# Four changes of order in a fused attention and GELU-MLP kernel: a value load, one set of transposes, a batch's loads and its row sums

## The chip, the cores and the metric

The kernel runs on one core of a Trainium2 chip. The metric is device time in microseconds (us) of one launch. The core's engines are TensorE (PE, matrix multiplication; its weight loads are shown as PEld), VectorE (DVE), ScalarE (ACT), GpSimd (POOL) and SyncE (SP). SP issues most of the DMAs, POOL those that change the type on the way.

## The reference, cut to what matters

```python
batch, n_heads, seq, head_dim = (8, 12, 448, 64)          # q, k, v in float32
q_n, k_n = (rmsnorm(q, g_q), rmsnorm(k, g_k))             # x / sqrt(mean(x*x) + 1e-6) * g
scores = (1.0 / np.sqrt(64)) * np.matmul(q_n, k_n.transpose(0, 1, 3, 2))
attn = softmax(scores)                                    # sum + 1e-9 in the divisor
x = np.matmul(attn, v).transpose(0, 2, 1, 3).reshape(3584, 768)
h = x @ w_in                                              # w_in 768 x 2048
g = gelu_tanh(h)
out = g @ w_out                                           # w_out 2048 x 768, float32
```

## The kernel before, in words

**Tiling.** A batch has 448 rows (4 groups of 112) and 12 heads, treated as 6 *pairs* of heads (two heads fill 128 lanes) and as 3 *chunks* of 4 heads. Batches are counted from 0 here, as in the code: "batch 1" of the change's short name is batch 0, its "batch 2" is batch 1, its "batch 3" is batch 2. `(b, c)` below is chunk c of batch b.

**Stages.** For each batch q and k are loaded chunk by chunk (`loads(b, c)`: one DMA for q, one for k, issued by SP, 448 KB each). The squares are made (`square`, on POOL or ACT), summed along each head's 64 elements (`total`, a DVE reduction), turned into 1/rms (`rsqrt` on ACT, or `rsqrt_pow` with a power on POOL), multiplied in (`normed`, on POOL or DVE), and transposed so that the head's 64 elements lie on the lanes. Transposing goes through TensorE and two DVE copies (`trans`, whole batch 0 and chunk 0 of batch 1), or through a DMA transpose that SP issues (`transposed(b, c)`: one for q, one for k), after which DVE multiplies the gain into the keys (`gain`). Buffers for q and k rotate over four tiles each; the squares of one tag (`sq`) over two.

**Attention of one batch** (`attention(b, ...)`) runs over 12 *slots*: slot 2p and 2p+1 belong to pair p. In a slot, the functions of a hand-written list (`side`) are issued first, then two blocks of `scores` (PE, followed by an exponential on ACT). An even slot also holds `pair_sums` of the pair before: with `what` = 0 the sums of the exponentials (PE, "ones") and their reciprocal, spread over the lanes by three DVE instructions (L253 to L255); with `what` = 1 the product with v (PE) and the scaling to x, written to `xT` (DVE, L248). Between them PE works off the second MLP multiplication of the batch before (`m2`, L283), whose results DVE copies to `osb` (L294) every 16 matmuls. At slot 11 `rsqrt` of the next batch but one is issued on ACT ahead of the slot's exponentials.

**Batch 0** has an attention of its own (`first_attention`) with four hand-written lists per slot: `side` ahead of the slot, `mid` between its two score blocks, `early` after them and ahead of `pair_sums`, `late` behind it. Here pair p+1 is transposed on PE at slot 2p+1, and one half of `pair_sums` of the pair before runs in each slot. POOL issues the loads of v (`load_v`, which converts to bf16) and the four halves of the MLP weights (`w_in_part`, `w_out_part`), between its squares and normalizations. Behind it comes the first MLP multiplication of batch 0 in pairs (`mm1_pair`, 8 steps), with its own list (`m1`, slots 0 to 7), and then `attention(1)`, whose `side` list is written in the loop's `b == 0` branch.

**Order.** Every engine works its own instructions in the order in which this program issues them; nothing is reordered by a scheduler (`manual_schedule`). An instruction that waits holds up everything behind it on its engine. A DMA starts when the issuing engine (SP or POOL) reaches it.

Of the kernel before, what the change touches and what calls it, by code (L numbers as in the profile page):

```python
# [16 lines left out]
def kernel(  # L17
# [11 lines left out]
    nc = tc.nc  # L29
# [7 lines left out]
    HP = H // 2  # L37
    CH = 4
    NCH = H // CH
# [17 lines left out]
    ps_m = ctx.enter_context(tc.tile_pool(name="ps_m", bufs=2, space=bass.MemoryType.PSUM))  # L57
# [32 lines left out]
    def load(b, c, n, parts=1, eng=nc.sync):  # L90
        t = rawqk.tile([P, CH, NK, D], F32, tag=f"raw{n}", name=f"raw{n}")
        src = {"q": q, "k": k}[n]
        raws[n, b, c] = t
        m = CH // parts
        return [
            lambda i=i: eng.dma_start(
                t[:, i * m:(i + 1) * m],
                src[b, c * CH + i * m:c * CH + (i + 1) * m].rearrange(
                    "h (p t) d -> p h t d", t=NK
                ),  # L100
            )
            for i in range(parts)
        ]

    def loads(b, c):
        for n in "qk":
            for go in load(b, c, n):
                go()

    def load_v(b, h, n):  # L110

        nc.gpsimd.dma_start(
            vb[b % 2][:, h:h + n], v[b, h:h + n].rearrange("h (p t) d -> p h t d", t=NK)
        )

    def square(b, c, n, eng, hs=slice(0, CH)):
        if (n, b, c) not in sqs:
            sqs[n, b, c] = stp.tile([P, CH, NK, D], F32, tag="sq", name="sq")
        sq, raw = sqs[n, b, c][:, hs], raws[n, b, c][:, hs]
        if eng is nc.scalar:  # L120
            nc.scalar.activation(sq, raw, AF.Square)  # L121
        else:
            eng.tensor_mul(sq, raw, raw)  # L123

    def total(b, c, n, hs=slice(0, CH)):
        if b not in sss:
            sss[b] = smp.tile([P, NCH, 2, CH, NK], F32, tag="ss", name="ss")
        nc.vector.reduce_sum(  # L128
            sss[b][:, c, "qk".index(n), hs], sqs[n, b, c][:, hs], axis=AX.X
        )  # L130
# [34 lines left out]
    def trans(b, hp, home=None):  # L165

        c, j = hp // (CH // 2), hp % (CH // 2)
        if hp == 0:
            qT[b] = qkp.tile([128, HP, S], BF16, tag="qT", name="qT")
        if home is ps_m:  # L170
            tp = ps_m.tile([128, 2, 512], BF16, tag="mm", name="tp")
        else:
            tp = ps_s.tile([128, 2, 1024], BF16, tag="sc", name="tp")
        for i, n in enumerate("qk"):
            for t in range(NK):
                nc.tensor.transpose(
                    tp[:, i, t * P:(t + 1) * P],
                    nrms[n, b, c][:, j, t].rearrange("p a d -> p (a d)"),
                    ident[:P, :P],
                )  # L180
        if b == 0 and hp == 0:
            nc.scalar.copy(qT[b][:, hp], tp[:, 0, :S])
        else:
            nc.vector.tensor_copy(qT[b][:, hp], tp[:, 0, :S])
        nc.vector.tensor_scalar(
            kT[:, hp, :, :P], tp[:, 1, :S].rearrange("p (t s) -> p t s", s=P), gcol[:, 0:1],
            None, op0=ALU.mult,
        )
# [249 lines left out]
    def pair(hp):  # L438
        return hp // (CH // 2), hp % (CH // 2), slice(2 * (hp % (CH // 2)), 2 * (hp % (CH // 2)) + 2)

    def squares0(hp, eng):
        c, _, hs = pair(hp)
        for n in "qk":
            square(0, c, n, eng, hs)

    def totals0(hp):
        c, _, hs = pair(hp)
        for n in "qk":
            total(0, c, n, hs)
# [5 lines left out]
    def normed0(hp, eng):  # L455
        c, j, _ = pair(hp)
        for n in "qk":
            normed(0, c, n, j, eng)

    def w_in_part(i, n):  # L460
        m = d_ff // n
        nc.gpsimd.dma_start(
            win[:, :, i * m:(i + 1) * m],
            moe_w_in[:, i * m:(i + 1) * m].rearrange("(c p) f -> p c f", p=128),
        )
# [34 lines left out]
    load_v(0, 0, 2)  # L500
    square(0, 1, "k", nc.gpsimd, slice(0, 2))
    load_v(0, 2, 4)
    w_in_part(0, 2)
    total(0, 1, "q", slice(0, 2))

    def pool_waits(b, c, n, j):
# [3 lines left out]
    side = [(1, lambda: normed0(1, nc.vector), lambda: pool_waits(0, 0, "k", 1),  # L510
             lambda: squares0(3, nc.gpsimd), lambda: total(0, 1, "k", slice(0, 2)),
             lambda: loads(1, 0)),
            (2, lambda: rsqrt0(2), lambda: normed0(2, nc.gpsimd),
             lambda: squares0(4, nc.gpsimd), lambda: totals0(3)),
            (4, lambda: normed0(3, nc.gpsimd), lambda: squares0(5, nc.gpsimd),
             lambda: totals0(4), lambda: loads(1, 1)),
            (6, lambda: normed0(4, nc.gpsimd), lambda: load_v(0, 6, 6),
             lambda: w_in_part(1, 2), lambda: totals0(5)),
            (8, lambda: normed0(5, nc.gpsimd),
             lambda: square(1, 0, "q", nc.gpsimd), lambda: square(1, 0, "k", nc.gpsimd),  # L520
# [2 lines left out]
             lambda: load_v(1, 0, CH), lambda: w_out_part(1)),  # L523
            (11, lambda: square(1, 1, "k", nc.gpsimd), lambda: square(1, 2, "q", nc.gpsimd))]
    mid = [(0, lambda: rsqrt0(1))] + [(2 * hp - 3, lambda hp=hp: rsqrt0(hp)) for hp in range(3, HP)]
    early = [(2 * hp + 1, lambda hp=hp: trans(0, hp + 1, ps_m)) for hp in (0, 2, 3, 4)]
    late = [(3, lambda: trans(0, 2, ps_m)), (9, lambda: total(1, 0, "q"))]
    first_attention(plan(*side), plan(*mid), plan(*early), plan(*late))
    def normed1(c):
        for j in range(CH // 2):  # L530
# [3 lines left out]
    def transposed(b, c):  # L534
        for n in "qk":
            dma_trans(b, c, n)
# [12 lines left out]
    for b in range(B):  # L549
        m1, side = [], []  # L550
        if b == 0:
            m1 = [(1, lambda: normed1(0), lambda: total(1, 1, "q"), lambda: total(1, 1, "k"),
                   lambda: load_v(1, CH, 2 * CH), lambda: rsqrt_pow(1, 1),
                   lambda: normed_all(1, 1)),
                  (2, lambda: total(1, 2, "q"), lambda: total(1, 2, "k"),
                   lambda: rsqrt_pow(1, 2), lambda: normed_all(1, 2)),
                  (3, lambda: trans(1, 0, ps_m)),
                  (4, lambda: trans(1, 1, ps_m), lambda: transposed(1, 1))]
            side += [(0, lambda: transposed(1, 2), lambda: loads(2, 0), lambda: loads(2, 1),
                      lambda: loads(2, 2)),  # L560
                     (2, lambda: gain(1, 1)), (5, lambda: gain(1, 2))]
            for c in range(NCH):
                side += [
                    (2 * c + 1, lambda c=c: square(2, c, "q", nc.gpsimd)),
                    (2 * c + 1, lambda c=c: square(2, c, "k", nc.gpsimd)),
                    (2 * c + 5, lambda c=c: total(2, c, "q")),
                    (2 * c + 6, lambda c=c: total(2, c, "k")),
                ]
        elif b + 1 < B:
            for c in range(NCH):  # L570
                m1 += [(0, lambda c=c: normed_all(b + 1, c)),
                       (4 * c + 4, lambda c=c: transposed(b + 1, c))]
            m1 += [(9, lambda: gain(b + 1, 0)), (14, lambda: gain(b + 1, 1))]
            side.append((3, lambda: gain(b + 1, 2)))
        if 0 < b and b + 2 < B:
            m1 += [(4, lambda: loads(b + 2, 1)), (8, lambda: loads(b + 2, 2))]
            for c, at in ((0, 1), (1, 9)):
                for i, (n, half) in enumerate((n, half) for n in "qk" for half in range(2)):
                    m1.append((at + i, lambda c=c, n=n, half=half: squared(b + 2, c, n, half)))
                m1 += [(at + 2, lambda c=c: total(b + 2, c, "q")),  # L580
                       (at + 4, lambda c=c: total(b + 2, c, "k"))]
            for n, slot in (("q", 1), ("k", 2)):
                m1.append((13, lambda n=n: square(b + 2, 2, n, nc.gpsimd)))
                side.append((slot, lambda n=n: total(b + 2, 2, n)))
        m1 = plan(*m1)
        for f in range(nf // 2 if b == 0 else nf):
            if b > 0:
                mm1(b, f)
            elif f > 1:
                mm1_pair(f)  # L590
            for fn in m1.get(f, ()):
                fn()
        m2 += m2_parts(b)
        if b + 1 == B:
            for fn in m2:
                fn()
            break
        nc.scalar.preload_act_table_set(EXP_SET)  # L598
        if b + 2 < B:
            side += [(11, lambda: rsqrt(b + 2)),  # L600
                     (0, lambda: load_v(b + 2, 0, H))]
            if b + 3 < B:
                side.append((1, lambda: loads(b + 3, 0)))
        attention(b + 1, m2, 96 if b == 0 else 112, plan(*side))
# [30 lines left out]
```

## Time and profile before

| | us |
|---|---|
| median of 3 runs | 454.71 (453.57 to 454.72) |
| profiled execution | 454.61 |
| its span, first to last instruction | 452.8 |
| PE busy | 433.3 (96%) |
| ACT busy | 303.6 (67%) |
| DVE busy | 249.8 (55%) |
| POOL busy | 168.3 (37%) |
| mean granted TensorE clock | 0.991 |

The time outside the span is 454.61 - 452.8 = 1.81 us. Busy time of PE contains pipelined matmuls with modelled ends, so 96% doesn't mean that PE is at its peak. A row of the timeline gives start, duration, engine, source line, operation, output<-input with its shape, count, and in brackets how long the engine stood idle just before and what released it. The rows of DMA issues give the tile, the issuing queue, the size and the time from issue to landing.

### The profile page before, as it was taken

To read this page: it belongs to the slowest core of one execution; us is meant where nothing else is said; L and a number is where in the kernel's file an instruction comes from. 1 tells how busy PE (TensorE), PEld (TensorE's weight loads), DVE (VectorE), ACT (ScalarE), POOL (GpSimd) and SP (SyncE) were. 2 spreads that over 40 slices of the span, in tenths; PEclk is the share of its full clock that TensorE was granted. 3 is DMA by queue.
4 is the path that set the end of the run, shared out by engine and by line. 5 is a ranking of instruction groups with operands and counts; after the bars stand their busy time and mean duration, and the time that the engine had idled before them with its cause. 6 is when DMAs were issued, how large, how long until landed. Compare 5 with 4: busy or idle time off the path is not lost.

```text
span 452.8 us, 7158 instructions
## 1 busy us (share of the span) xinstructions
PE 433.3 (96%) x2835; PEld 217.1 (48%) x2835; DVE 249.8 (55%) x426; ACT 303.6 (67%) x404; POOL 168.3 (37%) x142
## 2 busy tenths in 40 slices
PE   7778999799999999999999999999999999999995
PEld 3333544355445554455544554455544554555563
DVE  5777604772588436872388536873398603871000
ACT  5885469557889468856888478866888448863400
POOL 5998691873401921064400922055400910000000
PEclk9998999899999999999999999999999999999999
DMA  7999999929931768118941787217851521111022
GB/s 222 245 241 208 203 110 193 214 69 206 231 61 37 174 147 171 42 36 218 207 72 36 162 158 143 71 36 177 148 92 35 115 45 36 36 35 36 0 71 69
DMA packets 80754, 54.47 MB, mean 120 GB/s; under 512 B 39248, under 2 KB 75600, under 8 KB 80720
## 3 DMA queue, kind: packets, MB, share of 16 engines
q1 hardware_dynamic: 63936, 42.22, 39.0%
q0 software_dynamic: 16624, 11.80, 17.8%
q8 instruction: 22, 0.36, 0.3%
q14 instruction: 12, 0.10, 0.1%
q10 hardware_dynamic: 160, 0.00, 0.0%
HBM read 45.61 MB, written 11.01 MB: 125 GB/s over the span
## 4 chain that ended last, share of the span: by engine, by line
PE 73%; POOL 9%; ACT 6%; DVE 5%; DMA 3%; issue 2%; SPq 0%; ACTq 0%; DVEq 0%; POOLq 0%
PE h L262 28%; PE o L283 26%; PE o L241 11%; PE sc L214 7%; ACT ex L218 4%; DVE ss L128 3%; POOL rinv L147 2%; DMA rawk<-in_k_dram 2%; ACT L598 1%; POOL nrmk L159 1%; DVE es L229 1%; POOL g L123 1%; POOL sq L123 1%; POOL nrmq L159 1%; DMA grow<-in_g_k_dram 1%
## 5 line engine op out<-in xcount | busy, mean ns | idle before, releaser
L218 ACT ACTIVATE ex<-sc,shift 112x896 bf16<-112x896 f32 x192 | 182.7, 1003 | 32.4 <-PE sc L214 31.3
L283 PE MATMUL o<-wout,g 128*128 128x384 bf16 (+1 forms) x956 | 162.3, 329 | 0.0
L262 PE MATMUL h<-xT,win 128*128 128x448 bf16 x672 | 128.3, 352 | 0.0
L283 PEld LDWEIGHTS <-g 128*128 128x128 bf16 (+1 forms) x956 | 81.7, 99 | 71.0 <-issue 24.4
L266 ACT ACTIVATE g<-h 128x448 bf16<-128x448 f32 x112 | 60.9, 544 | 75.7 <-PE h L262 72.8
L262 PEld LDWEIGHTS <-win 128*128 128x128 bf16 x672 | 65.8, 98 | 61.0
L159 POOL TENSOR_TENSOR nrmq<-rawq,rinv 112x512 bf16<-112x512 f32 x44 | 46.8, 1082 | 127.1 <-issue 122.8
L128 DVE TENSOR_REDUCE ss<-sq 112x16 f32<-112x1024 f32 (+1 forms) x44 | 49.6, 1142 | 62.2 <-ACT sq L121 58.2
L294 DVE COPY osb<-o 128x384 f32<-128x384 f32 x52 | 28.7, 552 | 81.9 <-PE o L283 81.9
L214 PE MATMUL sc<-qT,kT 64*128 64x448 bf16 x384 | 58.0, 360 | 4.7 <-ACT ex L218 2.2
L241 PE MATMUL o<-ex,vb 112*64 112x448 bf16 x384 | 45.4, 356 | 4.0 <-DMA vb<-in_v_dram 3.3
L229 DVE TENSOR_TENSOR es<-ex 112x896 bf16<-112x896 bf16 x72 | 47.6, 662 | 2.7 <-ACT ex L218 1.7
L253 DVE STREAM_TRANSPOSE st<-o 128x448 f32<-128x448 f32 x48 | 31.1, 649 | 29.8 <-PE o L241 29.8
L159 POOL TENSOR_TENSOR nrmk<-rawk,rinv 112x512 bf16<-112x512 f32 x44 | 47.1, 1087 | 0.0
L214 PEld LDWEIGHTS <-kT 64*128 64x128 bf16 x384 | 17.3, 94 | 46.9 <-issue 40.3
L123 POOL TENSOR_TENSOR sq<-rawq 112x1024 f32<-112x1024 f32 x9 | 17.0, 1891 | 55.9 <-DMA rawq<-in_q_dram 28.3
L248 DVE TENSOR_TENSOR xT<-o,rb 128x448 bf16<-128x448 f32 x48 | 30.0, 625 | 9.3 <-PE o L241 4.7
L255 DVE STREAM_TRANSPOSE rb<-rc 128x448 f32<-128x448 f32 x48 | 31.0, 645 | 1.6
L241 PEld LDWEIGHTS <-vb 112*64 112x64 bf16 x384 | 23.2, 109 | 15.9 <-DMA vb<-in_v_dram 3.4
L241 PEld LDWEIGHTS <-ones 112*64 112x64 bf16 x240 | 15.0, 111 | 16.9 <-issue 11.2
L241 PE MATMUL o<-es,ones 112*64 112x448 bf16 x144 | 22.3, 358 | 0.6
L123 POOL TENSOR_TENSOR sq<-rawk 112x1024 f32<-112x1024 f32 (+1 forms) x11 | 19.5, 1771 | 1.9 <-POOL sq L123 0.8
(56 smaller groups left out, 216.4 us busy)
## 6 DMA issues: line engine op xcount, KB each, us to landing
rawq<-in_q_dram SPq DMA_DIRECT2D x22, 448.0 KB, 5.3
rawk<-in_k_dram SPq DMA_DIRECT2D x22, 448.0 KB, 6.2
vb<-in_v_dram POOLq DMA_DIRECT2D x6, 672.0 KB, 7.2
win<-in_moe_w_in_dram POOLq DMA_DIRECT2D x2, 1536.0 KB, 17.5
wout<-in_moe_w_out_dram POOLq DMA_DIRECT2D x2, 1536.0 KB, 19.3
out_dram<-osb SPq DMA_DIRECT2D x8, 336.0 KB, 2.8
out_dram<-osb SPq DMA_DIRECT2D x8, 288.0 KB, 2.7
out_dram<-osb SPq DMA_DIRECT2D x8, 240.0 KB, 2.7
```

Of the source, the lines that this page charges most:

```text
L123: eng.tensor_mul(sq, raw, raw)
L128: nc.vector.reduce_sum(sss[b][:, c, "qk".index(n), hs], sqs[n, b, c][:, hs], axis=AX.X)
L159: eng.tensor_mul(nrms[n, b, c][:, j].rearrange("p t a d -> p a t d"), raws[n, b, c][:, 2 * j:2 * j + 2], rinvs[b][:, c, "qk".index(n), 2 * ...
L214: nc.tensor.matmul(sc[:, a, :S], kT[r, hp, kt], qT[b][r, hp], start=True, stop=True,)
L218: nc.scalar.activation(exs[b, hp][:, kt], sc[:P, :, :S], AF.Exp, scale=scale, bias=shift)
L229: nc.vector.tensor_add(ess[b, hp][:, i], ex[:, 2 * i], ex[:, 2 * i + 1])
L241: nc.tensor.matmul(o[a * D:(a + 1) * D], vb[b % 2][:, 2 * hp + a, i] if what else ones, e[:, i, a], start=(i == 0), stop=(i == n - 1),)
L253: nc.vector.transpose(st.rearrange("p a b -> p (a b)"), o)
L255: nc.vector.transpose(oas["rb"], rc.to_broadcast([128, S // 32, 32]))
L262: nc.tensor.matmul(h[:, :S], win[:, c, f * 128:(f + 1) * 128], xT[b][:, c], start=(c == 0), stop=(c == HP - 1),)
L266: nc.scalar.activation(g[:, f, (b % 2) * S:(b % 2 + 1) * S], h[:, :S], AF.Gelu_apprx_tanh)
L283: nc.tensor.matmul(o[j * m:(j + 1) * m, :HD], g[:, f, i * 128 + j * m:i * 128 + (j + 1) * m], wout[:, f, half * HD:(half + 1) * HD], start ...
```

## The change

Four edits, all of them in hand-written lists.

1. The last six heads of batch 0's v are loaded ahead of the first half of `w_in`; that half is issued on POOL at slot 2, behind the normalization of pair 2.
2. In batch 0's attention the transposes of pair 2 are issued at slot 3 ahead of the product with v, as for the other pairs, and no longer behind it.
3. The six q and k loads of batch 2 are issued on SP at slots 5 and 6 of batch 0's first MLP multiplication, ahead of the DMA transposes of batch 1's chunk 2; before, they were issued behind these, at slot 0 of `attention(1)`. Loads and transposes share SP's queue.
4. The six `total` reductions of batch 2 are issued at slots 3, 5, 7, 9, 10 and 11 of `attention(1)`; before, at 5, 6, 7, 8, 9 and 10. The squares stay where they were (slots 1, 3, 5, on POOL).

```diff
     load_v(0, 2, 4)
-    w_in_part(0, 2)
+    load_v(0, 6, 6)
     total(0, 1, "q", slice(0, 2))
...
             (2, lambda: rsqrt0(2), lambda: normed0(2, nc.gpsimd),
-             lambda: squares0(4, nc.gpsimd), lambda: totals0(3)),
+             lambda: w_in_part(0, 2), lambda: squares0(4, nc.gpsimd), lambda: totals0(3)),
...
-            (6, lambda: normed0(4, nc.gpsimd), lambda: load_v(0, 6, 6),
+            (6, lambda: normed0(4, nc.gpsimd),
              lambda: w_in_part(1, 2), lambda: totals0(5)),
...
-    early = [(2 * hp + 1, lambda hp=hp: trans(0, hp + 1, ps_m)) for hp in (0, 2, 3, 4)]
-    late = [(3, lambda: trans(0, 2, ps_m)), (9, lambda: total(1, 0, "q"))]
+    early = [(2 * hp + 1, lambda hp=hp: trans(0, hp + 1, ps_m)) for hp in range(HP - 1)]
+    late = [(9, lambda: total(1, 0, "q"))]
...
-                  (4, lambda: trans(1, 1, ps_m), lambda: transposed(1, 1))]
-            side += [(0, lambda: transposed(1, 2), lambda: loads(2, 0), lambda: loads(2, 1),
-                      lambda: loads(2, 2)),
+                  (4, lambda: trans(1, 1, ps_m), lambda: transposed(1, 1)),
+                  (5, lambda: loads(2, 0), lambda: loads(2, 1)), (6, lambda: loads(2, 2))]
+            side += [(0, lambda: transposed(1, 2)),
                      (2, lambda: gain(1, 1)), (5, lambda: gain(1, 2))]
-            for c in range(NCH):
-                side += [
-                    (2 * c + 1, lambda c=c: square(2, c, "q", nc.gpsimd)),
-                    (2 * c + 1, lambda c=c: square(2, c, "k", nc.gpsimd)),
-                    (2 * c + 5, lambda c=c: total(2, c, "q")),
-                    (2 * c + 6, lambda c=c: total(2, c, "k")),
-                ]
+            for c, slots in enumerate(((3, 5), (7, 9), (10, 11))):
+                for n, slot in zip("qk", slots):
+                    side += [(2 * c + 1, lambda c=c, n=n: square(2, c, n, nc.gpsimd)),
+                             (slot, lambda c=c, n=n: total(2, c, n))]
```

## The prediction

> **What bounds the kernel now.** I read the page first: its chain of waits is mostly PE, with POOL, ACT, DVE and DMA together under a quarter.
>
> ```profile
> PE 73%; POOL 9%; ACT 6%; DVE 5%; DMA 3%; issue 2%; SPq 0%; ACTq 0%; DVEq 0%; POOLq 0%
> ```
>
> The edits end with batch 2's preparation, inside `attention(1)`; what comes later is only shifted by them. So I read PE's timeline up to there for its gaps, each with what ended it.
>
> ```profile
> 20.01 0.55 PE L214 MATMUL sc<-qT,kT 64*128 64x448 bf16 x4 [0.88 <-DVE kT L185]
> ...
> 34.87 1.25 PE L241 MATMUL o<-ex,vb 112*64 112x448 bf16 x8 [3.28 <-DMA vb<-in_v_dram]
> ...
> 84.29 0.95 PE L241 MATMUL o<-ex,ones 112*64 112x448 bf16 x8 [1.99 <-DVE st L253]
> 85.98 1.16 PE L241 MATMUL o<-ex,vb 112*64 112x448 bf16 x8 [0.74 <-DVE xT L248]
> ...
> 97.44 0.95 PE L241 MATMUL o<-ex,ones 112*64 112x448 bf16 x8
> ```
>
> The MLP of batch 0 lies between:
>
> ```profile
> 42.20 1.12 PE L314 MATMUL hh<-xT,win 128*128 128x448 bf16 x5
> ```
>
> Two stalls: one in batch 0's attention, on v, and one in `attention(1)`, on DVE. DVE's timeline says what DVE waited for there, and gives the step sizes I need.
>
> ```profile
> 76.88 0.44 DVE L204 TENSOR_SCALAR kT<-kT,gcol 128x896 bf16<-128x896 bf16 x1
> 80.15 1.22 DVE L128 TENSOR_REDUCE ss<-sq 112x16 f32<-112x1024 f32 x1 [2.83 <-POOL sq L123]
> 82.46 1.22 DVE L128 TENSOR_REDUCE ss<-sq 112x16 f32<-112x1024 f32 x1 [1.09 <-POOL sq L123]
> 83.59 0.64 DVE L253 STREAM_TRANSPOSE st<-o 128x448 f32<-128x448 f32 x1
> ...
> 85.84 1.21 DVE L128 TENSOR_REDUCE ss<-sq 112x16 f32<-112x1024 f32 x1
> 86.97 0.55 DVE L294 COPY osb<-o 128x384 f32<-128x384 f32 x1
> 87.43 1.21 DVE L128 TENSOR_REDUCE ss<-sq 112x16 f32<-112x1024 f32 x1
> ```
>
> From start to start: a pair's chain 2.25 us (83.59 to 85.84), a total 1.13, an osb copy 0.46. The two totals wait for POOL's squares, and those (POOL's and SP's timelines) for loads of batch 2 that SP issues behind a DMA transpose.
>
> ```profile
> 48.72 5.47 POOL L147 TENSOR_TENSOR rinv<-ms,mhalf 112x32 f32<-112x32 f32 x1 [5.47 <-DVE ms L145]
> ...
> 67.92 1.04 POOL L112 DMA_DIRECT2D vb<-in_v_dram  x1
> ```
>
> ```profile
> 58.34 1.24 SPq L199 DMA_TRANSPOSE kT<-nrmk  x1
> ...
> 68.00 1.22 SPq L199 DMA_TRANSPOSE kT<-nrmk  x1
> 69.27 0.57 SPq L96 DMA_DIRECT2D rawq<-in_q_dram  x1
> ...
> 75.94 1.50 SPq L96 DMA_DIRECT2D rawk<-in_k_dram  x1
> ```
>
> **Edits 1 and 2: v and the third pair's transposes.** The rows that price them, POOL's, DVE's and the landing times of the old v load (issued at 25.73) and of the first `w_in` half (issued at 12.23):
>
> ```profile
> 12.23 0.86 POOL L462 DMA_DIRECT2D win<-in_moe_w_in_dram  x1
> ...
> 16.24 1.03 POOL L159 TENSOR_TENSOR nrmk<-rawk,rinv 112x512 bf16<-112x512 f32 x1
> ...
> 25.73 0.83 POOL L112 DMA_DIRECT2D vb<-in_v_dram  x1
> ```
>
> ```profile
> win<-in_moe_w_in_dram POOLq DMA_DIRECT2D x1, 1536.0 KB, 18.9
> ...
> vb<-in_v_dram POOLq DMA_DIRECT2D x1, 336.0 KB, 9.1
> ```
>
> v now lands at 25.73 + 9.1 = 34.8, just when PE moves. Issued at 12.2 in `w_in`'s place it would land in the twenties, so 3.28 us goes, and the eight matmuls behind it lose 0.3 (1.25 against 0.95 at full clock). Pair 2's transposes ahead of the product with v remove the 0.88 gap, since DVE copies the keys while PE multiplies; I take 0.7, because POOL's next normalization comes 0.86 later (the `w_in` issue now stands ahead of it). Sum 4.3 us from the first stage on. Cover for `w_in`: issued near 17.3 (behind 16.24 + 1.03) with the old 18.9 it lands at 36.2; the MLP multiplication begins at 42.2 - 4.3 = 37.9. Everything up to 62 then runs 4.3 earlier, as what feeds it (DVE's normalization, then POOL's power at 48.72) follows PE and DVE.
>
> **Edits 3 and 4: loads and totals.** The old stall disappears if the loads land early: SP issues them behind T1 (the DMA transposes of batch 1's chunk 1; chunk 2's are T2), from 58.34 + 1.24 - 4.3 = 55.3 instead of 69.27. Gone would be 1.99 + 0.74 us and a slow clock. One half-us window of engine use behind the stall, with the granted clock third from its end:
>
> ```profile
> 87.00:87.50 0.50, 0.50 (x6) 0.13 (x4) 0.50 (x3) 0.00 (x0) 0.37 (x1) 0.50 1.10 242
> ```
>
> It stays at 0.50 in the windows from 87.0 to 89.5. There a run of PE takes up to twice as long; 1.4 us is my estimate for some 3 us of it, less than half as some of PE's work there waits for others. By the Trainium skill, "TensorE: Matmul & The Clock Gate", Part 1, the clock falls after an idle window of about 3.4 us; by that these two short gaps would cost their 2.73 us alone, and the trace differs: 0.50 after gaps of 1.99 and 0.74.
>
> But the loads now stand in SP's queue ahead of T2. T2's gain is issued on DVE at slot 5, in the old run at 76.88, now due at 76.88 - 4.3 = 72.6. If T2 is later, DVE stands, and behind it all of pairs 2 to 4, the totals and the `rsqrt` that ACT issues ahead of its last exponentials. So the question is when T2's keys land. DMA issues and queue traffic in windows carry it; landing times first, of the issues at 58.34, 75.94, 106.28 (a load) and 108.18 (the transpose behind it):
>
> ```profile
> kT<-nrmk SPq DMA_TRANSPOSE x1, 6.6
> ...
> rawk<-in_k_dram SPq DMA_DIRECT2D x1, 448.0 KB, 12.5
> ...
> rawk<-in_k_dram SPq DMA_DIRECT2D x1, 448.0 KB, 5.3
> ...
> kT<-nrmk SPq DMA_TRANSPOSE x1, 5.0
> ...
> kT<-nrmk SPq DMA_TRANSPOSE x1, 6.5
> ```
>
> The last is T2 itself, 68.00 + 6.5 = 74.5; T1 landed at 64.9, batch 2's last load at 88.4. At 106.28 the load landed at 111.6, the transpose behind it at 113.2, 1.6 later. Next the packets of POOL's queue (q0) and SP's (q1), in 57.5 to 59, then q1 in 59 to 65, both in 74.5 to 79.5, and q1 in 80 to 88:
>
> ```profile
> q0 software_dynamic: 514, 0.27, 130.5%
> q1 hardware_dynamic: 69, 0.02, 26.4%
> ...
> q1 hardware_dynamic: 1787, 0.44, 99.4%
> ...
> q1 hardware_dynamic: 1281, 1.27, 94.4%
> q0 software_dynamic: 285, 0.14, 20.0%
> ...
> q1 hardware_dynamic: 2013, 1.99, 108.8%
> ```
>
> *T1.* While q0 still moves weights, T1 gets 69 packets in 1.5 us, 46 per us; its bulk, 1787, moves once q0 runs dry near 59.5. Issued 4.3 earlier it is stuck all the same. Upper bound 64.9, as before. Lower bound, with the bulk behind 59.5 at the pace of a transpose alone (67 to 68, below): 61.4. By the nearest row, 4.3 us more at 46 give 200 packets, 0.6 us of a bulk that took nearly 6. So 64.3.
>
> ```profile
> q1 hardware_dynamic: 926, 0.23, 101.8%
> ```
>
> *The six loads.* Before, from T2's landing at 74.5 to 88.4, 13.9 us. New is that all of batch 2's v (672 KB, about 1340 packets, issued at 67.92 - 4.3) falls into them rather than the last 285 packets. That costs nothing by one row (q1 moved 256 packets per us beside q0, 252 alone), and by q0's own pace of 514 in 1.5 us, for some 1060 packets, 3.1. I take 0.6, near the row in which both run. They end at 64.3 + 13.9 + 0.6 = 78.8.
>
> *T2's keys* 1.6 behind that: L = 80.4. Lower bound 61.4 + 13.9 + 1.6 = 76.9, or 75.7 with six loads of 448 packets at 252 per us and 2 us of tail. Upper bound: 64.9 + 13.9 + 3.1 + 1.6 = 83.5, and 85 if T2 suffers beside v as it did in the old run (6.5 us, v issued at 67.92, against 5.0 of the one at 108.18).
>
> *From L to the end of the stage.* DVE has in order: gain 0.44, the second total, pair 2, a total, osb, pair 3, two totals, pair 4, the last total: 0.44 + 5 x 1.13 + 3 x 2.25 + 0.46 = 13.3. POOL's squares are ready in time, as each waits only for the total two before it. Then ACT:
>
> ```profile
> 93.17 0.37 ACT L137 ACTIVATE lg<-ss,eps 112x96 f32<-112x96 f32 x1 [0.46 <-DVE ss L128]
> ...
> 93.76 1.89 ACT L218 ACTIVATE ex<-sc,shift 112x896 bf16<-112x896 f32 x2
> ```
>
> 0.6 us from the total's end to the exponentials and 1.9 for two of them: 15.9 us after L. Pair 5's sums end 0.45 behind that, at L + 16.35; in the old run they ended at 97.44 + 0.95 = 98.4. So the change of time is L - 82.0, and with L = 80.4 it is -1.6. How much the first stage gains no longer matters: up to about 3 of its 4.3 us could be missing, and L would stand, because the queue sets it. Against the profiled execution, 454.61 - 1.6 = 453.0; the median stands 0.1 above that execution, so 453.1.
>
> What edit 4 adds by itself: the last total now stands behind pair 4 on DVE, so `rsqrt` and the last exponentials wait for it; without a late T2 this would cost 0.8 at pair 5's sums. Nothing else waits: POOL's normalization of batch 2 starts 1 us closer to its use, and its first transpose is held by output stores anyway.
>
> **The rivals.** *Full gain* (10%): T2 lands by 74, and both stalls go: 4.3 + 2.7 + 1.4 - 0.5 = 7.9, time 446.8. For it: alone a transpose needs one us. Against: the one at 108.18 landed only behind the load ahead of it.
>
> *Half gain* (20%): the queues share better than 46 packets per us. T1 is through by 61 to 63, v costs nothing, L = 76 to 79, change -6 to -3: 448.7 to 451.7. A rule of the Trainium skill gives this case, "DMA: Bandwidth & Descriptors", Queues, rings and completion order: an engine takes turns between queues, packet by packet. With half of the 583 packets per 1.5 us from 57.7 - 4.3 = 53.4 on, T1's 1787 end at 62.6, L is 78.7 and the time 451.4. The row of 69 against 514 speaks against it for transposes; 1281 beside 285 decides nothing.
>
> *Slower* (25%): T2 is starved beside v. v's full 3.1 us and 0.5 to 1.5 of starvation put L at 84 to 85: change +2 to +3, time 456.7 to 457.7. It decides from L = 83.4. For it: T2's 6.5 us in the old run, beside v. Against: here v has 14 us to pass ahead of T2.
>
> **How the numbers follow.** About 0.3%, 1.4 us, is what a measurement of this kernel can tell from no change. The forecast (45%) spans L from 78.9 to 83.4, the bound of faster, L = 80.6, near its middle: 23% of faster and 22% of same. With the rivals: faster 0.53, same 0.22, slower 0.25. The forecast's own range is 451.6 to 456.1. For 8 in 10 the range leaves out the full gain and the worst of starvation: 448.5 to 457.0.
>
> **What would show it.** Right: no wait for v near 31, the MLP of batch 0 beginning 4 us earlier, no wait of DVE for squares in `attention(1)`, but a DVE wait of 5 to 9 us ahead of L204 there, named a DMA; PE gaps at pair 4's scores; T2's keys landing near 80. Wrong: T2 landing by 75, or T1 by 61; wrong on the other side: a PE wait for `w_in` ahead of L314 near 38, T2 beyond 83, or the totals still waiting for POOL.

## The result, and the profile after

The changed kernel took **450.53 us** (median of 5 runs, 449.68 to 451.04), the kernel before, beside it on the same chip, 453.99 (452.68 to 454.72): a ratio of 0.9917, interval [0.9892, 0.9942], 3.5 us less. The profiled execution took 451.04 with a span of 449.3, 3.57 less than the profiled one of before.

First PE's timeline of the changed kernel, the rows that answer to those of before (start, duration, engine, line, operation, output<-input, count, and in brackets the idle time just before and its releaser):

```profile
30.47 0.95 PE L241 MATMUL o<-ex,vb 112*64 112x448 bf16 x8
...
38.88 8.29 PE L314 MATMUL hh<-xT,win 128*128 128x448 bf16 x43 [0.24 <-DVE xT L248]
...
79.02 0.55 PE L214 MATMUL sc<-qT,kT 64*128 64x448 bf16 x4 [2.27 <-DVE kT L204]
80.70 1.71 PE L241 MATMUL o<-ex,ones 112*64 112x448 bf16 x8 [1.13 <-DVE st L253]
...
92.30 1.62 PE L283 MATMUL o<-wout,g 128*128 128x384 bf16 x9 [0.61 <-DVE osb L294]
93.85 0.95 PE L241 MATMUL o<-ex,ones 112*64 112x448 bf16 x8
```

There is no wait for v at 30.47, and no wait for `w_in`. The main run of batch 0's MLP starts at 38.88; the row that answers to it in the old trace starts at 43.81:

```profile
43.81 8.29 PE L314 MATMUL hh<-xT,win 128*128 128x448 bf16 x43 [0.49 <-DVE xT L248]
```

So the first stage gained 4.9 us on PE, and the end of pair 5's sums, 98.4 before, is at 93.85 + 0.95 = 94.8: 3.6 are left. The rest went into PE's gaps in `attention(1)`: 2.27 + 1.13 + 0.61 = 4.0 us, where 1.99 + 0.74 = 2.7 stood before. DVE's timeline shows where the first of them comes from:

```profile
62.86 0.66 DVE L204 TENSOR_SCALAR kT<-kT,gcol 128x896 bf16<-128x896 bf16 x1 [1.15 <-DMA kT<-nrmk]
...
68.36 1.22 DVE L128 TENSOR_REDUCE ss<-sq 112x16 f32<-112x1024 f32 x1 [0.64 <-POOL sq L123]
...
78.51 0.45 DVE L204 TENSOR_SCALAR kT<-kT,gcol 128x896 bf16<-128x896 bf16 x1 [6.22 <-DMA kT<-nrmk]
```

DVE stands for 6.22 us ahead of the gain of chunk 2, from 72.3 on (the prediction had this turn at 72.6 and a wait of 5 to 9), as T2's keys land at 78.5. PE's gap of 2.27 us at pair 4's scores follows. The old waits for squares, 2.83 and 1.09 us, have shrunk to 0.64. ACT's timeline shows the end of the stage, where ACT waits for the last total:

```profile
91.81 0.38 ACT L137 ACTIVATE lg<-ss,eps 112x96 f32<-112x96 f32 x1 [3.58 <-DVE ss L128]
...
92.41 1.89 ACT L218 ACTIVATE ex<-sc,shift 112x896 bf16<-112x896 f32 x2
```

PE waits for the same total at its last gap, the 0.61 us above: the `osb` copy that it needs stands right behind that total on DVE. So both ways to pair 5's sums lead through DVE's list.

```profile
90.57 1.21 DVE L128 TENSOR_REDUCE ss<-sq 112x16 f32<-112x1024 f32 x1
91.70 1.01 DVE L294 COPY osb<-o 128x384 f32<-128x384 f32 x2
```

The answers on DMA issues give the landing times behind T1's keys (issued at 55.78), the last of the six loads (62.57) and T2's keys (67.70):

```profile
kT<-nrmk SPq DMA_TRANSPOSE x1, 7.1
...
rawk<-in_k_dram SPq DMA_DIRECT2D x1, 448.0 KB, 8.7
...
kT<-nrmk SPq DMA_TRANSPOSE x1, 10.8
```

That is 62.9, 71.3 and 78.5. Last the packets of the two queues in 62 to 70 and in 71 to 76:

```profile
q1 hardware_dynamic: 2817, 2.69, 110.1%
...
q0 software_dynamic: 1154, 0.59, 88.2%
q1 hardware_dynamic: 1207, 0.30, 50.0%
```

The first row is 352 packets per us, but it holds the last of T1's too; from 63 on, the loads alone ran at 342, with nothing of v beside them. T2 then ran beside all of v, in equal turns.

### The profile page after: what moved, and what is told of

Read it like the earlier page. It is cut to its first block, busy times and chain, and to the rows that moved or that the text cites. A ratio compares the mean times of both kernels' runs of the same rounds, so it can differ in the third digit from the quotient of the medians.

```text
span 449.3 us, 7158 instructions
## 1 busy us (share of the span) xinstructions
PE 432.5 (96%) x2835; PEld 217.4 (48%) x2835; DVE 251.9 (56%) x426; ACT 303.7 (68%) x404; POOL 168.8 (38%) x142
## 4 chain that ended last, share of the span: by engine, by line
PE 70%; POOL 12%; DVE 7%; ACT 4%; DMA 4%; issue 2%; SPq 0%; DVEq 0%; POOLq 0%
PE h L262 28%; PE o L283 25%; PE o L241 10%; PE sc L214 7%; DVE ss L128 4%; POOL g L123 3%; POOL rinv L147 2%; DMA kT<-nrmk 2%; ACT ex L218 2%; POOL nrmk L159 2%; POOL nrmq L159 2%; ACT L596 1%; POOL sq L123 1%; DVE es L229 1%; DMA rawq<-in_q_dram 1%
## 5 line engine op out<-in xcount | busy, mean ns | idle before, releaser
L159 POOL TENSOR_TENSOR nrmq<-rawq,rinv 112x512 bf16<-112x512 f32 x44 | 46.9, 1083 | 126.8 <-issue 123.0
L159 POOL TENSOR_TENSOR nrmk<-rawk,rinv 112x512 bf16<-112x512 f32 x44 | 47.1, 1089 | 0.0
L214 PEld LDWEIGHTS <-kT 64*128 64x128 bf16 x384 | 17.4, 93 | 48.8 <-issue 40.3
```

What stands on the lines that cost most here:

```text
L159: eng.tensor_mul(nrms[n, b, c][:, j].rearrange("p t a d -> p a t d"), raws[n, b, c][:, 2 * j:2 * j + 2], rinvs[b][:, c, "qk".index(n), 2 * ...
L214: nc.tensor.matmul(sc[:, a, :S], kT[r, hp, kt], qT[b][r, hp], start=True, stop=True,)
```

## The experiments

All runs are compared with the kernel before on their own chip (medians of 453.48 to 453.71 there). L is, as in the prediction, the landing of T2's keys.

**Each pair of edits alone.** The kernel before with edits 1 and 2 (first stage) in one run, with edits 3 and 4 (loads and totals) in the other; their diffs are the two halves of the change's own.

> Kernel before with edits 1 and 2 alone (v and the third pair's transposes); batch 2's loads and totals stay as before. In the trace after, batch 0's MLP began 4.9 us earlier and POOL's power 2.6 us earlier. My theory (the end of the stage is set by the landing of the DMA transposes of batch 1's chunk 2 in the changed kernel, and by POOL's squares in this one): the wait for v is gone, the DVE wait for squares stays at 2 to 4 us and moves 2.6 to 4.9 us earlier, so the time falls by 2.6 to 4.5 us, about as much as with all four edits (3.5). Rival (edits 3 and 4 bring most of the 3.5 us): at most -1.5 us here.

> Kernel before with edits 3 and 4 alone (loads of batch 2 ahead of the transposes, one total per division); v lands late as before. My theory (the stage ends 16.35 us after L, the landing of chunk 2's transposed keys, and L hangs on the queues, not on when PE arrives): the wait for v of 3.3 us stays, chunk 1's transposes land at 63 to 65, L is 78.5 to 80.5 and the time falls by 1.5 to 3.5 us. Rival (the first stage's gain is what is seen at the end, and edits 3 and 4 trade one stall for an equal one): 0 +- 1 us here.

Edits 1 and 2 alone: 451.82, ratio 0.9959 [0.9942, 0.9976], 1.9 us. DVE's and PE's rows:

```profile
77.30 1.22 DVE L128 TENSOR_REDUCE ss<-sq 112x16 f32<-112x1024 f32 x1 [4.62 <-POOL sq L123]
79.31 1.22 DVE L128 TENSOR_REDUCE ss<-sq 112x16 f32<-112x1024 f32 x1 [0.79 <-POOL sq L123]
...
81.14 1.70 PE L241 MATMUL o<-ex,ones 112*64 112x448 bf16 x8 [3.70 <-DVE st L253]
```

That is less than the 2.6 to 4.5 expected and a little over the rival's 1.5. Part of the first stage's gain went into the old stall: DVE's first wait for squares grew from 2.83 to 4.62 and PE's gap from 1.99 to 3.70.

Edits 3 and 4 alone: 450.8, ratio 0.9938 [0.9918, 0.9957], 2.8 us.

```profile
35.08 1.33 PE L241 MATMUL o<-ex,vb 112*64 112x448 bf16 x6 [3.20 <-DMA vb<-in_v_dram]
...
78.36 0.45 DVE L204 TENSOR_SCALAR kT<-kT,gcol 128x896 bf16<-128x896 bf16 x1 [0.63 <-DMA kT<-nrmk]
...
94.00 0.95 PE L241 MATMUL o<-ex,ones 112*64 112x448 bf16 x8
```

The wait for v is still there, and yet T2 lands at 78.3, as in the full change (78.5), and the times agree within their spread. The two halves don't add: with both, what the first stage gains becomes DVE's wait for T2, 0.63 here and 6.22 there. The queue sets L, not the first stage. The run doesn't show that L sets the end: PE, which comes late here, has no gap from pair 4's scores to pair 5's sums, so its own work ends at the same place, 94.95, as L + 16.6.

**What holds T2 up.** Two kernels on the base of the change, and one with both edits. Batch 2's v behind T2:

```diff
-                      (0, lambda: load_v(b + 2, 0, H))]
+                      (8 if b == 0 else 0, lambda: load_v(b + 2, 0, H))]
```

> Changed kernel, with batch 2's v issued on POOL at slot 8 of attention(1) instead of slot 0, so that it moves after the transposes. In the trace after, the six loads had moved by 70 and the transposes of chunk 2 moved from 70 to 77 beside v's packets, one for one. Theory A (v beside the transposes makes them late): they land at 72 to 73, the DVE wait ahead of the gain (6.2 us) falls under 1.5 us, pair 5's sums end near 89.5 instead of 94.8, the time falls to 8 to 9 us under the kernel before. Rival B (the loads ahead of them in SP's queue make them late): they land at 77 or later, the wait stays over 4 us, time as the changed kernel within 1 us. Rival C (DVE's list of totals is the limit, whatever the transposes do): wait gone, but time within 1.5 us of the changed kernel.

Four of the six loads behind T2:

```diff
-                  (5, lambda: loads(2, 0), lambda: loads(2, 1)), (6, lambda: loads(2, 2))]
-            side += [(0, lambda: transposed(1, 2)),
+                  (5, lambda: loads(2, 0))]
+            side += [(0, lambda: transposed(1, 2), lambda: loads(2, 1), lambda: loads(2, 2)),
```

> Changed kernel, with only chunk 0's two loads of batch 2 ahead of the transposes of batch 1's chunk 2, the other four behind them as before; v at slot 0 as in the change, totals as in the change. Rival B (the loads ahead make the transposes late): they land by 69 to 70, no DVE wait ahead of the gain, totals of chunk 1 and 2 just in time, time 7 to 9 us under the kernel before. Theory A (v beside the transposes makes them late): they start before v's first packets at 70, so they are through by 70 here too, and the time is the same 7 to 9 under, unless the four loads beside v come too late for the squares, which would show as a DVE wait for POOL at slots 9 to 11 of 1 to 4 us. Rival C (DVE's list of totals is the limit): within 1.5 us of the changed kernel.

> Changed kernel with both moves: four of batch 2's six loads behind the transposes of batch 1's chunk 2, and batch 2's v at slot 8. Nothing lies ahead of these transposes but two loads, and nothing beside them. Theory A (the stage ends 16.4 us after the later of their landing and the gain's turn): they land at 67 to 69, DVE doesn't wait for them, the gain comes at its turn near 72.2 (73.1 with v alone moved), pair 5's sums end near 88.6, time 0.5 to 1 us under the kernel with v alone moved (7.8 us under before). Rival D (the loads' slow pace of 250 packets per us in the kernel before, against 345 in the changed one, comes with standing behind a transpose): the four loads move at 230 to 260 per us here too. Theory E (the slow pace comes when v's packets stretch the end of the transpose ahead of the loads): 330 to 350 here.

| kernel | us | ratio | T2's keys land | pair 5's sums end |
|---|---|---|---|---|
| changed | 450.53 | 0.9917 [0.9892, 0.9942] | 78.5 | 94.8 |
| v behind | 445.71 | 0.9827 [0.9811, 0.9844] | 73.0 | 89.4 |
| four loads behind | 446.92 | 0.9848 [0.9828, 0.9868] | 72.4 | 89.8 |
| both | 445.83 | 0.9831 [0.9811, 0.9851] | 67.7 | 89.2 |

With v behind, T2's packets in 71 to 72 and DVE's gain:

```profile
q1 hardware_dynamic: 1092, 0.27, 128.4%
...
73.08 0.45 DVE L204 TENSOR_SCALAR kT<-kT,gcol 128x896 bf16<-128x896 bf16 x1 [1.16 <-DMA kT<-nrmk]
...
88.42 0.95 PE L241 MATMUL o<-ex,ones 112*64 112x448 bf16 x8
```

1092 packets in one us, against 241 per us beside v: **v beside T2 was worth 5.5 us of L**, and 4.8 of the time by the medians, 4.1 by the ratios ((0.9917 - 0.9827) x 454). The end keeps its distance, 89.37 - 73.0 = 16.4. Either edit removes most of the wait, though the time fell by 7.8 us with v behind, where 8 to 9 was expected, and by 6.6 with four loads behind, where it was 7 to 9: there DVE waits 0.93 us for a square, as the late loads feed POOL late. With both, T2 lands 5 us earlier still and nothing follows, where 0.5 to 1 us was expected. L is then no longer the bound, since DVE reaches the gain only at 71.6; the rule of the fixed distance ends near L = 73.

In the run with both, the four late loads have no v beside them either and still went at about 250 packets per us (1762 in 68 to 75), where the changed kernel's went at 342. So v doesn't explain the two paces of loads of the same shape.

```profile
q1 hardware_dynamic: 1762, 1.75, 106.0%
```

**The totals.** The changed kernel with the totals at their old slots 5 to 10, and the version with both edits above with the totals at 3, 5, 7, 8, 9 and 10.

> Changed kernel with the totals of batch 2 at the old slots (5 to 10) and all else as changed: edit 3 without edit 4. Theory A (DVE's list from the landing at 78.4 on sets the stage): the first total joins the list (+1.1 us) and pair 4 leaves it ahead of the last total (-2.3), so ACT's rsqrt comes 1.1 us earlier and the time is 0.5 to 1.1 us under the changed kernel, unless PE's own work behind pair 3 holds pair 5's sums. Rival F (one total per slot is what makes the changed kernel fast): 1 us or more slower than the changed kernel.

> The kernel with both moves and the last totals earlier: slots 3, 5, 7, 8, 9, 10, so that ACT's rsqrt doesn't stand behind pair 4's chain on DVE. Theory A: the 3.3 us for which ACT waits for the last total in the kernels with v moved shrink to under 1.5, pair 5's sums follow PE's own work, the time is 0 to 0.8 us under the kernel with both moves. Rival G (the squares come too late for totals at slots 8 to 10): DVE waits 1 to 2 us for POOL there and the time is 0.5 us or more over it.

With old slots: 451.63, ratio 0.996 [0.9942, 0.9977], 1.1 us above the changed kernel as rival F had it, and not below it as theory A had it. T2 lands at 77.2, 1.3 earlier, but the sums end at 95.2, L + 18.0, 0.4 later.

```profile
77.25 0.45 DVE L204 TENSOR_SCALAR kT<-kT,gcol 128x896 bf16<-128x896 bf16 x1 [5.10 <-DMA kT<-nrmk]
...
77.76 0.55 PE L214 MATMUL sc<-qT,kT 64*128 64x448 bf16 x4 [0.88 <-DVE kT L204]
80.57 1.71 PE L241 MATMUL o<-ex,ones 112*64 112x448 bf16 x8 [2.25 <-DVE st L253]
```

Two totals now stand between the gain and the `st` that PE waits for, and PE's second gap is 2.25 instead of 1.13. ACT's last wait is gone, yet that pays nothing. The clock also fell for longer. Busy time by stretches, first the changed kernel, then this one (granted clock third from the end):

```profile
79.00:82.00 3.00, 1.85 (x12) 1.03 (x13) 2.83 (x5) 1.91 (x2) 1.83 (x1) 0.74 0.46 137
82.00:85.00 3.00, 3.00 (x19) 1.11 (x16) 2.93 (x6) 0.62 (x1) 1.53 (x2) 0.69 0.00 0
85.00:88.00 3.00, 2.89 (x26) 1.37 (x24) 2.90 (x4) 2.96 (x4) 1.07 (x2) 1.00 0.00 0
```

```profile
79.00:82.00 3.00, 1.43 (x8) 0.82 (x8) 2.83 (x5) 1.13 (x2) 3.00 (x2) 0.68 0.11 32
82.00:85.00 3.00, 3.00 (x15) 0.90 (x13) 3.00 (x5) 0.52 (x1) 2.25 (x2) 0.50 0.00 0
85.00:88.00 3.00, 3.00 (x16) 1.23 (x16) 2.83 (x5) 1.71 (x3) 2.15 (x2) 0.68 0.00 0
```

If the clock is either 1 or 0.5, its means give (0.26 + 0.31) x 3 x 2 = 3.4 us at half speed in the changed kernel, and (0.32 + 0.50 + 0.32) x 3 x 2 = 6.8 here.

The run with both edits and earlier totals: 446.1, ratio 0.984 [0.982, 0.986]; ACT's wait for the last total falls from 3.39 to 1.14, and the time stays (theory A had up to 0.8 us less). So edit 4's late last total costs nothing where T2 is early, as that wait lies off PE's path.

**T1 and the weights ahead of it.** The changed kernel with the second half of `w_out` issued behind batch 1's normalizations:

```diff
-             lambda: load_v(1, 0, CH), lambda: w_out_part(1)),
+             lambda: load_v(1, 0, CH)),
...
-                   lambda: normed_all(1, 1)),
+                   lambda: normed_all(1, 1), lambda: w_out_part(1)),
```

> Changed kernel with the second half of w_out issued on POOL behind the normalization of batch 1's chunk 1 (near 55.7) instead of at slot 10 of batch 0's attention, so that POOL's queue runs dry near 52 and the transposes of chunk 1, issued at 53.8 and 55.8, find it empty. In the trace after their first packets came at 57.5, 3.7 us behind the issue. Theory H (they are held off by POOL's saturated queue): first packets near 55, landing at 57 to 59 instead of 62.9. Rival I (something of their own holds them): first packets at 57 or later. The later w_out then shares with batch 2's loads, so L stays at 76 to 80 and the time within 2 us of the changed kernel.

453.43, ratio 0.9989 [0.9973, 1.0005], 2.9 us above the changed kernel, where it was to stay within 2. T1, with POOL's queue empty, starts about 1.2 us after its issue. Its keys land at 60.3 and not at 57 to 59: SP's queue moves nothing in 57 to 59, while `w_out` starts with 416 packets of POOL's queue. The six loads then share with `w_out` and v, T2 lands at 80.2, and the sums end at L + 16.4. The transfer that was taken from T1's way came back in the way of the loads.

The changed kernel, and the one with v behind T2, with DVE's normalization (L159) issued behind POOL's work on the next chunk, which frees POOL and T1 earlier:

```diff
-            m1 = [(1, lambda: normed1(0), lambda: total(1, 1, "q"), lambda: total(1, 1, "k"),
+            m1 = [(1, lambda: total(1, 1, "q"), lambda: total(1, 1, "k"),
...
-                   lambda: normed_all(1, 1)),
+                   lambda: normed_all(1, 1), lambda: normed1(0)),
```

> The changed kernel, with DVE's normalization of half a pair (nrmq, nrmk of batch 1's chunk 0) issued behind POOL's squares, power and normalizations of chunk 1 in the list instead of ahead of them. In the changed kernel these two took 1.36 and 2.38 us on DVE beside POOL's squares, 0.68 each before. Theory L (two-input operations of DVE and POOL hold each other up): DVE takes 0.6 to 0.8 us each when they no longer lie beside POOL's squares, and POOL's power, freed of the wait, begins at 42.5 to 44 instead of 46.2. Theory H (the DMA transposes T1 get no packet before POOL's queue of weights runs dry at 57.5): T1's first packets stay at 57 to 58 and its landing at 62.5 to 63.5 although it is issued 2 to 3 us earlier, and the time stays at 449.5 to 451.5. Rival R (T1's landing follows its issue): T1 lands by 61, L falls by 2 and the time to 448 to 449.

> The version with batch 2's v behind the transposes of chunk 2 (slot 8), with DVE's normalization moved as in the run beside it. Theory H: T1 and with it the loads and T2 move by less than 1 us, so that pair 5's sums end at 88.9 to 89.8 (89.4 without the move) and the time is 445.0 to 446.5. Rival R: L 71, sums' end 87.4 if no other wait takes over, time 443.7 to 444.5.

> The changed kernel itself, on the chip of the other runs of this call, as their base: 450.5, ratio 0.992 to the kernel before.

> The changed kernel with the totals at their old slots 5 to 10, for a second time, now on the same chip as the changed kernel. If its loss comes from the order of DVE's work (a total ahead of pair 4 leaves PE a second gap, and PE a second window at half clock): 451.3 to 452.0, 0.8 to 1.5 above the changed kernel, with about twice as much time at a granted clock under 0.75 in the 80s. If the difference was one of chips: within 0.5 of it.

These four ran on one chip. The changed kernel again: 450.52, 0.9934 [0.991, 0.9959]. Normalization last: 451.31, 0.9941 [0.9918, 0.9965]. v behind T2 and normalization last: 446.84, 0.9849 [0.9822, 0.9876]. Old totals again: 451.83, 0.995 [0.993, 0.997].

DVE's and POOL's rows, of the changed kernel (its first profile) and of normalization last:

```profile
39.49 2.36 POOL L123 TENSOR_TENSOR g<-rawq 112x1024 f32<-112x1024 f32 x1
...
40.02 2.38 DVE L159 TENSOR_TENSOR nrmk<-rawk,rinv 112x512 bf16<-112x512 f32 x1
...
46.16 5.47 POOL L147 TENSOR_TENSOR rinv<-ms,mhalf 112x32 f32<-112x32 f32 x1 [3.47 <-DVE ms L145]
```

```profile
41.99 0.73 DVE L159 TENSOR_TENSOR nrmk<-rawk,rinv 112x512 bf16<-112x512 f32 x1
...
42.25 5.81 POOL L147 TENSOR_TENSOR rinv<-ms,mhalf 112x32 f32<-112x32 f32 x1
...
50.21 1.32 SPq L199 DMA_TRANSPOSE qT<-nrmq  x1
...
64.59 0.45 DVE L204 TENSOR_SCALAR kT<-kT,gcol 128x896 bf16<-128x896 bf16 x1 [2.84 <-DMA kT<-nrmk]
```

Theory L was right: the multiplication takes 0.73 us clear of POOL's squares and 2.38 beside them, and POOL's power begins 3.9 us earlier, at 42.25. T1 is issued at 50.21 instead of 53.78, and it brought nothing: T1's keys land at 64.6, later than either theory had them, and the time is that of the changed kernel or slightly more (expected 449.5 to 451.5). On top of v behind T2 it brought nothing either: the sums end at 89.6, and 446.84 is 0.3 above the range. Theory H was right on the time and **wrong on its cause**. In the changed kernel POOL's queue is alone in 54 to 57 (first row), which H took for T1 being held off; with T1 issued earlier, its packets begin while POOL's queue is full, and in 54.5 to 57.5 the two take equal turns:

```profile
q0 software_dynamic: 885, 0.61, 134.3%
```

```profile
q0 software_dynamic: 564, 0.43, 90.7%
q1 hardware_dynamic: 564, 0.14, 36.3%
```

At 188 per us, T1 needs far longer than in the changed kernel, where it begins near 57.5 and soon has the queue to itself. About the same bytes pass ahead of T1's end in both, so the earlier issue moves nothing. Old totals again lost 1.3 us against the changed kernel beside them. Normalization last has nearly the same long fall of the clock, 6.7 us by the means below, and its sums end at 95.4, L + 17.4, where the changed kernel on this chip has 94.2, L + 16.3:

```profile
79.00:82.00 3.00, 1.14 (x12) 0.74 (x12) 2.83 (x6) 1.87 (x2) 1.89 (x1) 0.88 0.73 174
82.00:85.00 3.00, 3.00 (x15) 0.94 (x14) 2.85 (x5) 0.90 (x1) 1.89 (x1) 0.50 0.00 0
85.00:88.00 3.00, 3.00 (x13) 0.98 (x13) 2.88 (x3) 1.31 (x3) 1.15 (x1) 0.50 0.00 0
```

The 1.1 us between is DVE waiting for a PE that still runs at half speed, ahead of pair 4's last `st`:

```profile
88.96 0.65 DVE L253 STREAM_TRANSPOSE st<-o 128x448 f32<-128x448 f32 x1 [1.06 <-PE o L241]
```

The best version is the changed kernel with v behind T2: 445.71, 7.8 us under the kernel before on its chip (453.48). The one with both moves, 445.83, can't be told from it.

## Why the prediction was right or wrong

**The sign and the mechanism were right.** The old stalls on v and on squares go, T2's keys become late, and DVE's wait for them takes the place of the stall. The change of time was to be L - 82.0: with the measured 78.5 that is -3.5, and the profiles differ by 3.57. The sums' end was to be L + 16.35; it is L + 16.3, and with the change's order of totals it was 16.3 to 16.6 for L from 73.0 to 80.2, but for normalization last, where PE at half clock made it 17.4. That L wouldn't depend on the first stage was right too: edits 3 and 4 alone have the same L. That their time is the same as well is in part chance, as PE without a gap ends there too.

**L itself was sized wrong, in three terms that partly cancel.** Predicted 64.3 + 14.5 + 1.6 = 80.4; measured 62.9 + 8.4 + 7.2 = 78.5.

- *T1, 64.3 against 62.9.* I took 46 packets per us as T1's pace beside weights. That row, taken 1.2 to 2.7 us after an issue, was most likely a transpose's start and not its share: the first packets came about 3.8 us after the issue in the changed kernel, and about 4 where T1 was issued at 50.21. After that the turns were equal. What sets the length of the start stays open: in the old kernel, T1's first packets came 1.2 to 1.4 us after the issue, with POOL's queue busy too. The Trainium skill's rule ("DMA: Bandwidth & Descriptors", Queues, rings and completion order), an engine takes turns between queues packet by packet, agrees with 564 beside 564 and 1207 beside 1154; it doesn't show in the first microseconds behind an issue. By it I had 62.6 for T1's end, the better number; I gave it up for a row that showed something else.
- *The six loads, 13.9 + 0.6 against 8.4.* I carried over the pace of the loads of before, 252 packets per us; here it was 342, for a reason that no run shows. And v didn't fall into them. POOL issued it at 65.37, and q0 has no packet in 62 to 70. So the 0.6 went as well.
- *T2, 1.6 against 7.2.* The step "1.6 behind that" took T2's landing behind one load, with no other queue. v, which I had put beside the loads, came beside T2 and took every other packet. My rival on the slower side named this cause, T2 beside v, with 0.5 to 1.5 us as its price; it was 5.5, and only the fast loads kept the time from it.

So the measured time lies in the half gain, which had 20%, and below the forecast's own range, 451.6 to 456.1. The wider range of 448.5 to 457.0 held it. Half gain had assumed better sharing and free v; it came out by fast loads and a dear v. That the three errors of L, -1.4, -6.1 and +5.6, leave only -1.9 is luck.

**The first stage** gained 4.9 us at PE, not 4.3. But "everything up to 62 then runs 4.3 earlier" failed behind it: POOL's power came only 2.6 earlier (46.16 against 48.72), since DVE's normalization now lay beside POOL's squares. It didn't matter for the reason given: the queue sets L.

**Edit 4.** The 0.8 of cost that I gave it without a late T2 isn't there: moving the last total forward changed ACT's wait by 2.3 us and the time by nothing that can be told. With a late T2 its order is even worth about 1.2 us (1.1 and 1.3 by two pairs of medians, which is near the limit of what can be told), and the rows name one total instead of two ahead of the `st` that PE waits for, and the shorter fall of the clock. How much each of them is worth wasn't separated. A long fall alone need not cost: with `w_out` behind it lasted 6.8 us too, at the changed order of totals, and the sums ended at L + 16.4. The order alone doesn't seem to cost the 1.3 us either: of the twelve executions of old totals again, the two with a mean granted clock of 0.999 and 1.0 took 449.86 and 449.65, less than the changed kernel's median; whether T2 came earlier in these two, no trace shows.

**The clock.** I had the half-speed window as 3 us; here too it is one of 3.4, so the change did not remove it, and its 1.4 us stayed out of the gain. It is gone where L is about 73 or less and in edits 3 and 4 alone, which have no such gap in PE.

## What to carry to other kernels

Before moving a load ahead of a transfer that someone waits for, list what each DMA queue will hold in that stretch and add up the packets of all queues, since here they shared in turns once both were moving; the move that paid most here was one of another queue's load, out of the way. A pace read from the first microseconds of a transfer is the pace of its start. Where a bound is a sum of landings, look at the chain behind it separately: it may hold well (16.3 to 16.6 here, but for one run) while the terms of the landing are off by 6 us each.

## What was not expected of the hardware

- In the three profiles shown, a stretch at half clock lasts 3.4 us or about twice that: 3.4 after gaps of 2.27 and 1.13, 6.8 after 0.88 and 2.25. The Trainium skill ("TensorE: Matmul & The Clock Gate", Part 1) has windows of about 3.4 us, which fits these lengths; that the clock falls after a whole idle window doesn't fit. By the mean of 0.74 in 79 to 82 it fell in the changed kernel near 80.4 (82.0 less 1.56 us at half speed), and PE had worked for 0.55 us from 79.02 on, within the 3.4 us ahead of that.
- A two-input DVE operation of 0.7 us took 2.38 beside POOL's squares, and the gain of 0.45 took 1.77 in the run with v and four loads behind T2, whose row follows (a square ran on POOL from 71.24 to 73.13). The Trainium skill ("SBUF — State Buffer", Who interferes with whom) has one port pair that the two engines lock for a whole instruction; the rows agree.

```profile
71.61 1.77 DVE L204 TENSOR_SCALAR kT<-kT,gcol 128x896 bf16<-128x896 bf16 x1
```

- What sets the pace of loads of one shape, 342 packets per us or 250, stays open. v beside them isn't it: in the changed kernel and in the one with both edits they had the queue to themselves. Batch 2's loads went at the fast pace where they stood ahead of T2 and at the slow one behind it, as rival D had it for the four late loads; but batch 3's first two loads, also behind T2, moved 655 packets in 78 to 80 in the changed kernel, 328 per us, so the place behind a transpose isn't the whole cause either.
